# Spreading step log decays on TensorE instead of by DMA, in an mLSTM and two-layer expert kernel

## The chip, the cores and the metric

One core of one Trainium2 chip runs the whole kernel. The metric is the device time of one execution in microseconds (us); lower is better. The runs before: 764.24, 759.52 and 763.80 us, median 763.8.

## The reference

Three layers follow each other. First an mLSTM over 4 batches, 8 heads, 768 tokens and head size 40 (batch x head = 32 rows), with exponential gates:

```python
for t in range(S):
    m_new = np.maximum(f_gate[:, :, t] + m, i_gate[:, :, t])
    f_stab = np.exp(f_gate[:, :, t] + m - m_new)
    i_stab = np.exp(i_gate[:, :, t] - m_new)
    C = f_stab * C + i_stab * einsum('bhd,bhe->bhde', vt, kt)
    n = f_stab * n + i_stab * kt
    y[:, :, t] = sigmoid(o_gate) * (C @ qt) / max(abs(n @ qt), 1)
```

Its 3072 tokens of 320 numbers then go through a mixture of 8 experts (the best of 8 logits picks one, with `relu` between two products and the softmax weight as a factor), and through a dense layer `(h * cos(h)) @ w_out` with `h = x @ w_in` of width 2048.

## The kernel before, in words

**The loop.** The mLSTM is computed in chunks of `L` = 128 tokens. A step `i` of the loop (`for i in range(NT)`, L1051, `NT` = 24) is chunk `c = i // 4` of batch `b = i % 4`, for all 8 heads (4 pairs, `NP`). Inside a chunk the recurrence is written with sums of log decays: `G` holds, for the 32 rows of batch and head, the running sum of the log of `f_stab` since the start of the chunk (`gate_scan`, L256). Step `i` needs, on all partitions, the row of `G` of each of its heads along the tokens: 64 partitions for the even head of a pair, 64 for the odd. This spread row is `gb`, 128 x 4 x 128 numbers.

**Where gb comes from.** For chunk 0, `spread_g` (L329) makes it by f32 matmuls: a column of the identity, repeated 64 times, picks a row of `G` and writes it to 64 partitions of a PSUM bank. For the later chunks `gate_scan` writes `G` to DRAM (`g_d`, L273 to L277), and `load_g` (L232) reads a row back into 64 partitions at once, two DMAs of 128 KB in a step, into one of three SBUF buffers `gb_t`.

**A step's work, in the order in which it is written.** `exps(i + 1)` (L400): eight exponentials of `gb` on ACT make the decay weights `P`, POOL masks them (L418), scales the keys (L422) and the old state (L432). `scores(i)` (L441): PE multiplies keys and queries into banks 0 and 1, DVE multiplies by `P` (L460). `values(i - 1)` (L464): PE makes the state's increment `ps` in bank 6 (L473, columns 0 to 163), the values in bank 4 (L480) and the old state's share in bank 5 (L488); DVE updates the state (L497), adds up and divides (L502 to L524), POOL finishes `y` (L526). Then come the loads of step `i + 3`, the logits of step `i - 3` (L547, bank 3, read by DVE in L548) and the transposes of step `i - 2` (L537, bank 2, copied by ACT to `xT`). Between DVE's operations `fill()` puts single operations of routing and ranking. In two steps of four one piece of `w_in` is decoded (L1723 to L1738), once the step's logits are done.

**What sets the order.** The schedule is by hand: each engine runs its instructions in the order in which they are written, and waits for what they need. All loads of the loop and the stores of finished tiles (`x_d`, L602) are issued by one queue, SP, in this order: gb, kvn, qk (two), v (two), stores. A PSUM bank is one tile `bk[n]`; `qk_t` and `kv_t` have four buffers, so that the load of step `i + 3` goes where step `i - 1` has read. The gates `G`, `gg` and `smask` lie in the space of `w2r`, whose weights come after the loop.

Of the kernel before, what the change touches and what calls it, by code (L numbers as in the profile page):

```python
# [8 lines left out]
F32 = mybir.dt.float32  # L9
F32R = mybir.dt.float32r  # L10
BF16 = mybir.dt.bfloat16
I32 = mybir.dt.int32
U32 = mybir.dt.uint32
AF = mybir.ActivationFunctionType
ALU = mybir.AluOpType
# [4 lines left out]
B, H, S, D = 4, 8, 768, 40  # L20
L = 128
NC = S // L
NP = H // 2
DM = H * D
NTOK = B * S
NT = NTOK // 128
E = 8
# [68 lines left out]
def kernel(  # L96
# [16 lines left out]
    nc = tc.nc  # L113
    V, A, G_, T_ = nc.vector, nc.scalar, nc.gpsimd, nc.tensor
    cp = ctx.enter_context(tc.tile_pool(name="cp", bufs=1))
    dp = ctx.enter_context(tc.tile_pool(name="dp", bufs=1, space=DRAM))
# [1 line left out]

    x_d = dp.tile([NTOK, DM], F32, name="x_d")
    x2_d = dp.tile([NTOK, DM + 1], F32, name="x2_d")  # L120
    g_d = dp.tile([NC - 1, 2, B * NP, L], F32, name="g_d")

    cst = cp.tile([128, C_W], F32, name="cst")
    w_ir = cp.tile([128, 3, DF2], F32, name="w_ir")
# [10 lines left out]
    bk = [pp.tile([128, 512], F32, name=f"bk{i}") for i in range(8)]  # L135
    ident = cst[:, C_ID:C_ID + 128]
# [5 lines left out]
    def pool(stack, name, side="left", bufs=1):  # L142
        return stack.enter_context(tc.tile_pool(name=name, bufs=bufs, side=side, reuse_waits="tile"))

    def many(p, n, name, *shape):
        return [p.tile([128, *shape], F32, name=f"{name}{i}") for i in range(n)]
# [7 lines left out]

    gl = pool(pl_, "gl", "right")
    ge = pool(pe_, "ge")
    NQ, NKV, NG, NPB = 4, 4, 3, 3
    kw_t = many(ge, 3, "kw", NP, 2, 64)
    gb_t = many(ge, 3, "gb", NP, L)
    qk_t = many(ge, 1, "qk", NP, 3 * L)  # L160
    kv_t = many(ge, 1, "kv", 2 * DM + H * DV)
    vb_t = many(ge, 2, "vb", 2, 2, NP * DV)
# [17 lines left out]
    gg, G, smask = (wf[0:B * H, n * S:(n + 1) * S] for n in range(3))  # L180
# [12 lines left out]
    HL, QO = L // 2, 3 * L // 2  # L193
    Z = (slice(0, HL), slice(HL, L))
# [17 lines left out]
    def run(g):  # L212
        for _ in g:
            pass
# [14 lines left out]
            nc.sync.dma_start(out=vb[Z[a], :, a], in_=vpair[i, a])  # L229
        vbt[i] = vb  # L230

    def load_g(i):  # L232
        c, b = divmod(i, B)
        gb = gb_t[i % NG]
        src = g_d[c - 1, :, b * NP:(b + 1) * NP].rearrange("a n t -> a (n t)")
        for a, z in enumerate(Z):
            nc.sync.dma_start(
                out=gb.rearrange("p n t -> p (n t)")[z], in_=src[a:a + 1].to_broadcast([HL, NP * L])
            )
        gbt[i] = gb  # L240

# [14 lines left out]
    def gate_scan(c0, c1, eng):  # L256

        lo, hi = c0 * L, c1 * L
        r, r1 = slice(lo, hi), slice(max(lo, 1), hi)
        r0 = slice(r1.start - 1, hi - 1)  # L260
        V.tensor_tensor_scan(
            out=mm[:, r], data0=fg[:, r], data1=ig[:, r], initial=mm[:, lo - 1:lo] if lo else -1e30,
            op0=ALU.add, op1=ALU.max,
        )
        yield
        V.tensor_tensor(out=gg[:, r1], in0=fg[:, r1], in1=mm[:, r0], op=ALU.add)
        yield
        V.tensor_tensor(out=gg[:, r1], in0=gg[:, r1], in1=mm[:, r1], op=ALU.subtract)
        yield
        V.tensor_tensor_scan(  # L270
            out=G[:, r], data0=smask[:, r], data1=gg[:, r], initial=0.0, op0=ALU.mult, op1=ALU.add
        )
        for a in range(2 if c0 else 0):  # L273
            nc.sync.dma_start(
                out=g_d[c0 - 1:c1 - 1, a].rearrange("c r t -> r c t"),
                in_=G[a:B * H:2, r].rearrange("r (c t) -> r c t", c=c1 - c0),
            )  # L277
        yield
        eng.tensor_tensor(out=aa[:, r], in0=ig[:, r], in1=mm[:, r], op=ALU.subtract)
        yield  # L280
        V.tensor_tensor(out=aa[:, r], in0=aa[:, r], in1=G[:, r], op=ALU.subtract)
        yield
        g3 = G[:, r].rearrange("r (c t) -> r c t", c=c1 - c0)[:, :, L - 1:L]
        V.tensor_tensor(
            out=a2[:, r].rearrange("r (c t) -> r c t", c=c1 - c0), in0=aa[:, r].rearrange("r (c t) -> r c t", c=c1 - c0),
            in1=g3.to_broadcast([B * H, c1 - c0, L]), op=ALU.add,
        )
        yield
        if c0:
            V.tensor_tensor(  # L290
                out=decr[:, c0:c1], in0=g3.to_broadcast([B * H, c1 - c0, B * NP]),
                in1=cst[:B * H, C_DM:C_DM + B * NP].unsqueeze(1).to_broadcast([B * H, c1 - c0, B * NP]),
                op=ALU.mult,
            )
            yield
# [237 lines left out]
    def xpose(i):  # L533
        y = yt[i]
        px = bk[2][:, 0:384]
        for k, c in enumerate(KC):
            T_.transpose(out=px[:, 128 * k:128 * k + 128], in_=y[:, c:c + 128], identity=ident)  # L537
        xT = xT_t[i % 2]
        A.activation(out=xT.rearrange("p k t -> p (k t)"), in_=px, func=AF.Copy)
        xTt[i] = xT  # L540

    def logits(i):
        xT = xTt.pop(i)
        pl = bk[3 if i < NT - 1 else 2][:, 0:E]
        for k in range(3):
            for z in (slice(0, 64), slice(64, 128)):
                T_.matmul(out=pl[z], lhsT=xT[:, k, z], rhs=wg[:, k, :], start=(k == 0), stop=(k == 2))  # L547
        V.tensor_tensor(out=lg[:, i, :], in0=pl, in1=bias[:, i, :], op=ALU.add)  # L548
        fill()
# [493 lines left out]
    nc.sync.dma_start(out=mb, in_=mbias)  # L1043
    nc.sync.dma_start(out=wg, in_=w_gate)
    gs = gate_scan(1, NC, G_)
    for _ in range(GS0):
        next(gs)
    load_qk(3)
# [2 lines left out]
    for i in range(NT):  # L1051
        if i == 0:
            scores(0)
            spread_g(1)
            exps(1)
            spread_g(2)
            for _ in range(5):
                next(gs)
            keep_warm(DUM)
        else:  # L1060
            exps(i + 1)
            if i >= 4 and i < NT - 1 and (i - 4) % B == B - 1 and (i - 4) // B >= SLOW:
                ex_exp((i - 4) // B)
            scores(i)
        if i >= 8 and i % B == 0 and i // B - 2 < SLOW:
            c = i // B - 2
            bg.append(in_turn(rank(c, rank_mm(c)), rows_of(c)))
        if i == NT - 2:
            run(e0)
            early_rows(0)  # L1070
            gather(0)
        if i >= 1:
            values(i - 1)
        if i == 1:
            spread_g(3)
        if 1 <= i <= B:
            keep_warm(DU2, 5)
        if i == 1:
            run(gs)
        if i == 2:  # L1080
            keep_warm(DU3, 2)
            rest()
            token_bias()
        if i == 3:
            natural(1, NC, G, eG, AF.Exp, bk[7])()
        if 3 < i + 3 < NT:
            load_g(i + 3)
            load_kv(i + 3)
            load_qk(i + 3)
            load_v(i + 3)  # L1090
        if i == B:
            nc.sync.dma_start(out=Rf.rearrange("p r e -> p (r e)"), in_=consts[:, C_R:C_END])
        if i == EARLY[0] + 4:
            run(wt[NC - 3])
            run(pf)
            e0 = early_slot(0, star)
            bg.append(e0)
        if i >= 3:
            logits(i - 3)
        if i >= 2:  # L1100
            xpose(i - 2)
        if i >= 3 and (i - 3) % B == B - 1:
            rt = route((i - 3) // B)
            bg.append(rt)
            if SLOW <= (i - 3) // B and i < NT - 2:
                run(rt)
        if i >= 4 and i < NT - 1 and (i - 4) % B == B - 1:
            c = (i - 4) // B
            if c < SLOW:
                run(rt)  # L1110
                ex_exp(c)
            weigh_later(c)
            if i == EARLY[0] + 3:
                pf = pick_first()
                bg.append(pf)
        if i >= 8 and i % B == 0 and i // B - 2 < SLOW:
            run(wt[i // B - 2])
            wq.append(weigh(i // B - 2))
        weigh_some(2 if i > EARLY[0] else 1)
        if 0 < i <= 4:  # L1120
            G_.memset(XS[:, i - 1], 0.0)
        if i >= 2:
            next(sp_ops, None)
        if i == EARLY[0] + 4:
            load_w(0, 0)
        if i == 2:
            next(dec_ops)
        if B <= i < EARLY[0] + 2 and i % B < 2:
            for _ in range(STEPS[i % 2]):
                next(dec_ops, None)  # L1130
        if i == NT - 2:
            for _ in dec_ops:
                pass
            pe_.close()
            pw_ = pool(ctx, "pw")
            wide(pw_, 0)
            hp = [[pw_.tile([128, 2, SLOT], F32R, name=f"{n}{k}") for k in range(2)] for n in ("hh", "hl")]
            for ts, t_ in zip((hh_t, hl_t), hp):
                ts += [t_[k % 2][:, k // 2] for k in range(NHB)]
            load_w(0, 1)  # L1140
# [449 lines left out]
    n = 4 * (DM + 68)  # L1590
# [4 lines left out]
    gp, gv, gg, gs_ = {}, {}, {}, {}  # L1595
# [218 lines left out]
```

## Time and profile before

| | us |
|---|---|
| median of three runs | 763.8 |
| the profiled execution | 765.02 |
| its span (first to last instruction) | 763.3 |
| PE busy | 712.1 (93%) |
| DVE busy | 525.4 (69%) |
| ACT busy | 390.7 (51%) |
| POOL busy | 208.7 (27%) |

The page gives busy time by engine, the span in 40 slices, and the costliest groups of instructions; the trace behind it can be asked for stretches, waits and single instructions. Engines: PE multiplies, PEld loads its weights, DVE and ACT work on vectors, POOL does vector work and indirect DMAs, SP issues DMAs; "SPq" is that queue. The mLSTM loop takes the first 160 us or so, experts and dense layer the rest. The mean granted clock of PE was 0.977 of full speed.

### The profile page before, as it was taken

Reading aid. Unit: us, or ns where it says so; the run is one execution under the profiler, and the core shown is the slowest. Engines: PE = TensorE matmul, PEld = TensorE weight load, DVE = VectorE, ACT = ScalarE, POOL = GpSimd, SP = SyncE. Lnnn points to the kernel's source line nnn. Section 1 sums busy time; section 2 is a strip of 40 time slices with the busy share of each in tenths; the row PEclk is TensorE's granted clock in tenths of the full one; section 3 lists DMA queues with packets and bytes.
Section 4 is the critical chain, followed back from the end, with each engine's and each line's share of the span. In section 5 each row is a group of like instructions: output and inputs, shape, how many; then the busy total and the mean of one; then the engine's idle time right before and its main releaser. Section 6 shows DMA issues by size and latency. Waiting matters only on the chain. (4 is left out here: it accounts for less than half of the span.)

```text
span 763.3 us, 16584 instructions
## 1 busy us (share of the span) xinstructions
PE 712.1 (93%) x5947; PEld 651.7 (85%) x5948; DVE 525.4 (69%) x1206; ACT 390.7 (51%) x903; POOL 208.7 (27%) x280
## 2 busy tenths in 40 slices
PE   8787888789999999999969999999999999999995
PEld 6677777778998999999957899998899998889994
DVE  8788786778445687665648877676677676767662
ACT  4547556544233465454546655555555555555451
POOL 8656566331154442332433002002002001001102
PEclk9899999879999999999999999999999999999998
DMA  7798988871063583422811010010010000000000
GB/s 192 195 230 221 249 234 241 228 214 54 19 194 98 150 251 107 120 75 76 282 44 66 1 36 35 0 35 35 1 35 34 2 1 22 14 1 10 26 1 35
DMA packets 48654, 73.74 MB, mean 97 GB/s; under 512 B 5518, under 2 KB 33776, under 8 KB 48560
## 3 DMA queue, kind: packets, MB, share of 16 engines
q1 hardware_dynamic: 41248, 50.48, 24.3%
q10 hardware_dynamic: 3664, 10.27, 4.7%
q0 software_dynamic: 3648, 11.82, 4.6%
q8 instruction: 49, 0.80, 0.5%
q14 instruction: 45, 0.37, 0.2%
HBM read 89.82 MB, written 12.22 MB: 134 GB/s over the span
## 5 line engine op out<-in xcount | busy, mean ns | idle before, releaser
L1626 ACT ACTIVATE w1r<-w1r 128x512 f32<-128x512 f32 x96 | 60.7, 632 | 104.2 <-DVE w1r L1621 97.9
L1628 DVE TENSOR_TENSOR w1r<-bk,w1r 128x512 f32<-128x512 f32 x96 | 66.3, 691 | 52.5 <-ACT w1r L1626 51.0
L1619 ACT ACTIVATE w1r<-bk,qtr 128x512 f32<-128x512 f32 x96 | 66.0, 687 | 57.8 <-PE bk L1614 55.2
L943 PE MATMUL bk<-XH,WIH 128*128 128x256 f32 x288 | 77.5, 298 | 3.9 <-DVE hl L950 2.5
L1620 DVE TENSOR_SCALAR w1r<-w1r 128x512 f32<-128x512 f32 x96 | 41.2, 429 | 53.0 <-ACT w1r L1619 51.1
L949 ACT ACTIVATE hh<-bk 128x256 fp32r<-128x256 f32 x96 | 36.6, 382 | 75.4 <-PE bk L943 57.8
L1646 PE MATMUL bk<-WOH,gh 128*128 128x320 f32 x228 | 71.0, 311 | 0.0
L1646 PE MATMUL bk<-WOH,gl 128*128 128x320 f32 x228 | 70.6, 310 | 0.0
L1621 DVE TENSOR_TENSOR w1r<-w1r 128x512 f32<-128x512 f32 x96 | 68.3, 711 | 3.3
L1646 PE MATMUL bk<-WOL,gh 128*128 128x320 f32 x228 | 70.4, 309 | 0.0
L950 DVE SCALAR_TENSOR_TENSOR hl<-bk,hh 128x256 fp32r<-128x256 f32 x96 | 40.1, 418 | 42.1 <-ACT hh L949 25.8
L1614 PE MATMUL bk<-XH,WIH 128*128 128x512 f32 x144 | 57.8, 401 | 4.8 <-issue 4.1
L943 PEld LDWEIGHTS bk<-XH,WIH 128*128 128x128 f32 x288 | 55.3, 192 | 7.2 <-DVE hl L950 3.7
L964 PE MATMUL bk<-WOH,hl 128*128 128x320 f32 x192 | 59.9, 312 | 1.2 <-DVE hl L950 1.2
L964 PE MATMUL bk<-WOH,hh 128*128 128x320 f32 x192 | 59.7, 311 | 0.0
L964 PE MATMUL bk<-WOL,hh 128*128 128x320 f32 x192 | 59.4, 309 | 0.0
L970 POOL DMA_INDIRECT x_d<-ys,cinv x26 | 29.3, 1127 | 103.6 <-ACTq L924 74.0
L1614 PE MATMUL bk<-XL,WIH 128*128 128x512 f32 x144 | 57.3, 398 | 0.0
L1614 PE MATMUL bk<-xh,WIH 128*128 128x512 f32 x144 | 56.5, 392 | 0.0
L1614 PE MATMUL bk<-xl,WIH 128*128 128x512 f32 x144 | 56.1, 389 | 0.0
L943 PE MATMUL bk<-XH,WIL 128*128 128x256 f32 x192 | 50.3, 284 | 0.0
L943 PE MATMUL bk<-XL,WIH 128*128 128x256 f32 x288 | 50.2, 284 | 0.0
(381 smaller groups left out, 1986.0 us busy)
## 6 DMA issues: line engine op xcount, KB each, us to landing
w2r<-in_w_dram SPq DMA_DIRECT2D x26, 640.0 KB
w1r<-in_w_dram SPq DMA_DIRECT2D x26, 512.0 KB
w1r<-in_w_dram SPq DMA_DIRECT2D x52, 128.0 KB
kvl<-in_kvn_dram SPq DMA_DIRECT2D x12, 484.0 KB
gb<-g_d SPq DMA_DIRECT2D x40, 128.0 KB
raw<-in_w_out_dram ACTq DMA_DIRECT2D x8, 640.0 KB
qkl<-in_qk_dram SPq DMA_DIRECT2D x24, 160.0 KB
x_d<-y SPq DMA_DIRECT2D x24, 160.0 KB
```

What stands on the lines that cost most here:

```text
L943: T_.matmul(out=ph, lhsT=a, rhs=x_, start=(n == 0), stop=(n == len(mms) - 1))
L949: A.activation(out=hh, in_=ph, func=AF.Relu)
L950: V.scalar_tensor_tensor(out=hl, in0=ph, scalar=0.0, in1=hh.bitcast(F32), op0=ALU.max, op1=ALU.subtract)
L964: T_.matmul(out=py(s, g), lhsT=a[:, gs], rhs=w_, start=(f == 0 and n == 0), stop=(f == NF - 1 and n == 2),)
L970: r = G_.indirect_dma_start(out=dst, out_offset=bass.IndirectOffsetOnAxis(ap=idx, axis=0), in_=src, in_offset=None, bounds_check=NTOK - 1, ...
L1614: T_.matmul(out=ph, lhsT=a, rhs=x_, start=(n == 0), stop=(n == len(mms) - 1))
L1619: A.activation(out=v, in_=gp[T, f], func=AF.Identity, bias=qtr, scale=1.0 / (2 * math.pi))
L1620: V.tensor_scalar(out=kk, in0=v, scalar1=MAGIC, scalar2=MAGIC, op0=ALU.add, op1=ALU.subtract)
L1621: V.tensor_tensor(out=v, in0=v, in1=kk, op=ALU.subtract)
L1626: A.activation(out=v, in_=v, func=AF.Sin, scale=6.283185)
L1628: V.tensor_tensor(out=g, in0=gp.pop((T, f)), in1=v, op=ALU.mult)
L1646: T_.matmul(out=po, lhsT=a[:, js], rhs=w_, start=(f == 0 and n == 0), stop=(f == NFC - 1 and n == 2),)
```

## The change

`g_d`, its writes, `load_g` and the three `gb_t` go. In steps 2 to 4 `g_parts` takes `G` of chunks 1 to 5 apart into three bf16 parts, the value, what is left of it, and what is left of that, stacked in `g3` (96 partitions: three times the 32 rows); `pick` holds the identity three times. `spread_later(i + 2)` then makes `gb` in step `i` in PSUM bank 3: for steps 4 to 6 (`i < FIRST`) by f32 matmuls as in `spread_g`, for the others by one bf16 matmul a head over 96 rows, which adds the three parts up. The logits move from bank 3 to columns 256 to 263 of bank 6 and behind the transposes.

```diff
-    g_d = dp.tile([NC - 1, 2, B * NP, L], F32, name="g_d")
-    NQ, NKV, NG, NPB = 4, 4, 3, 3
+    NQ, NKV, NPB = 4, 4, 3
+    FIRST = B + 3
-    gb_t = many(ge, 3, "gb", NP, L)
+    g3, gm = (ge.tile([128, S - L], BF16, name=n) for n in ("g3", "gm"))
+    pick = ge.tile([128, B * H], BF16, name="pick")
...
-    def load_g(i):
+    def g_parts():
+        g, r = G[:, L:], smask[:, L:]
+        BH = B * H
+        for k in range(3):
+            z = slice(k * BH, (k + 1) * BH)
+            A.activation(out=pick[z], in_=ident[z, z], func=AF.Copy)
+        A.activation(out=g3[0:BH], in_=g, func=AF.Copy)
+        G_.tensor_tensor(out=r, in0=g, in1=g3[0:BH], op=ALU.subtract)
+        yield
+        A.activation(out=gm[0:BH], in_=r, func=AF.Copy)
+        G_.tensor_tensor(out=r, in0=r, in1=gm[0:BH], op=ALU.subtract)
+        yield
+        A.activation(out=g3[BH:2 * BH], in_=gm[0:BH], func=AF.Copy)
+        A.activation(out=g3[2 * BH:3 * BH], in_=r, func=AF.Copy)
+        yield
+
+    def spread_later(i):
+
         c, b = divmod(i, B)
-        gb = gb_t[i % NG]
-        src = g_d[c - 1, :, b * NP:(b + 1) * NP].rearrange("a n t -> a (n t)")
-        for a, z in enumerate(Z):
-            nc.sync.dma_start(
-                out=gb.rearrange("p n t -> p (n t)")[z], in_=src[a:a + 1].to_broadcast([HL, NP * L])
+        gb = bk[3].rearrange("p (n t) -> p n t", n=NP)
+        if i < FIRST:
+            K, of, g = slice(0, B * H), ident, G[:, c * L:(c + 1) * L]
+        else:
+            K, of, g = slice(0, 3 * B * H), pick, g3[0:3 * B * H, (c - 1) * L:c * L]
+        for h in range(H):
+            r = b * H + h
+            T_.matmul(
+                out=gb[Z[h % 2], h // 2], lhsT=of[K, r:r + 1].to_broadcast([K.stop, HL]), rhs=g, start=True, stop=True
             )
         gbt[i] = gb
...
-        for a in range(2 if c0 else 0):
-            nc.sync.dma_start(
-                out=g_d[c0 - 1:c1 - 1, a].rearrange("c r t -> r c t"),
-                in_=G[a:B * H:2, r].rearrange("r (c t) -> r c t", c=c1 - c0),
-            )
...
-        pl = bk[3 if i < NT - 1 else 2][:, 0:E]
+        pl = bk[6][:, 256:256 + E] if i < NT - 2 else bk[3 if i < NT - 1 else 2][:, 0:E]
...
-            load_g(i + 3)
...
+        if 2 <= i < 5:
+            next(gp)
+        if B <= i + 2 < NT:
+            spread_later(i + 2)
+        if i >= 2:
+            xpose(i - 2)
         if i >= 3:
             logits(i - 3)
-        if i >= 2:
-            xpose(i - 2)
```

## Rows read from the trace of the kernel before

**Rows 1.** Stretches from the scores of steps 4, 8, 12, 16, 20 to 23; columns named.
```profile
core 0: us, PE busy (x) PEld busy (x) DVE busy (x) ACT busy (x) POOL busy (x), PEclk, DMA share, GB/s
33.40:60.80 27.40, 21.84 (x364) 19.64 (x365) 20.00 (x55) 14.07 (x46) 15.35 (x25) 0.90 0.96 233
60.80:85.20 24.40, 20.29 (x385) 18.23 (x386) 19.39 (x58) 14.99 (x48) 15.07 (x24) 1.00 0.90 230
85.20:109.10 23.90, 21.66 (x386) 19.63 (x386) 20.10 (x65) 14.26 (x45) 16.11 (x25) 0.93 0.87 239
109.10:133.60 24.50, 21.94 (x392) 19.92 (x392) 15.99 (x61) 14.71 (x47) 14.27 (x25) 0.93 0.89 241
133.60:155.50 21.90, 17.94 (x269) 16.29 (x270) 15.36 (x57) 10.34 (x33) 7.47 (x11) 0.84 0.79 221
```

**Rows 2.** Waits of the loop, 20 to 190 us: total us, times, longest.
```profile
ACT Pl L409 <- DMA gb<-g_d: 20.3, 10, 4.0
...
PE bk L448 <- DMA qk<-in_qk_dram: 8.4, 3, 4.0
```

**Rows 3.** Queue SP, issues of the loads of step 12 and a store.
```profile
75.88 1.67 SPq L237 DMA_DIRECT2D gb<-g_d  x2
...
78.27 0.83 SPq L218 DMA_DIRECT2D qk<-in_qk_dram  x1
...
81.32 1.55 SPq L602 DMA_DIRECT2D x_d<-y  x1
```

**Rows 4.** Timeline of PE, step 9: start us, us, engine, line, tiles, count.
```profile
67.29 0.68 PE L448 MATMUL bk<-qkb 128*128 128x128 f32 x4 [1.08 <-DVE rk L661]
...
69.21 0.62 PE L473 MATMUL bk<-kv,kw 128*64 128x41 f32 x16
...
71.32 0.23 PE L488 MATMUL bk<-M,qk 128*64 128x82 f32 x1
...
72.17 0.61 PE L448 MATMUL bk<-qkl 128*128 128x128 f32 x4
```

**Rows 5.** Timeline of DVE, steps 8 to 10, state update and logits.
```profile
65.47 0.66 DVE L497 TENSOR_TENSOR Ml<-Mc,bk 40x164 f32<-40x164 f32 x2 [1.59 <-PE bk L488]
...
69.08 0.16 DVE L548 TENSOR_TENSOR lg<-bk,bias 128x8 f32<-128x8 f32 x1
...
71.60 0.65 DVE L497 TENSOR_TENSOR M<-Mc,bk 40x164 f32<-40x164 f32 x2
...
74.55 0.12 DVE L548 TENSOR_TENSOR lg<-bk,bias 128x8 f32<-128x8 f32 x1
...
77.25 0.65 DVE L497 TENSOR_TENSOR M<-Mc,bk 40x164 f32<-40x164 f32 x2
```

**Rows 6.** Timeline at the start of the loop: SP and PE.
```profile
20.74 1.28 SPq L274 DMA_DIRECT2D g_d<-w2r  x2
...
26.51 0.86 SPq L218 DMA_DIRECT2D qk<-in_qk_dram  x1
...
33.41 1.19 PE L448 MATMUL bk<-qk 128*128 128x128 f32 x4 [3.96 <-DMA qk<-in_qk_dram]
```

**Rows 7.** Timeline, prices of kinds: f32 spread, exponentials, subtraction, copy.
```profile
7.50 1.97 ACT L409 ACTIVATE P<-bk,aw 128x128 f32<-128x128 f32 x8 [0.42 <-PE bk L332]
...
9.50 1.96 PE L332 MATMUL bk<-w2r,cst 32*64 32x128 f32 x32
...
16.97 1.54 POOL L279 TENSOR_TENSOR w1r<-w1r 32x640 f32<-32x640 f32 x1
...
66.31 0.49 ACT L539 ACTIVATE xT<-bk 128x384 f32<-128x384 f32 x1 [0.82 <-PE bk L537]
...
68.47 2.24 ACT L409 ACTIVATE Pl<-gb,aw 128x128 f32<-128x128 f32 x8 [0.43 <-DMA gb<-g_d]
```

**Rows 8.** Timeline: ACT held in step 20, PE held at the first slot.
```profile
136.80 1.02 ACT L601 ACTIVATE y<-y,gate 128x320 f32<-128x320 f32 x2 [3.41 <-DVE gate L595]
...
165.71 1.33 PE L844 MATMUL bk<-cst,XS 128*128 128x128 f32 x5 [3.44 <-DMA XS<-x_d,inv]
```

More of the change, by code (lines that the diff above doesn't have):

```diff
@@ L1045 @@
     gs = gate_scan(1, NC, G_)
+    gp = g_parts()
     for _ in range(GS0):
```

## The prediction

> **What bounds the kernel now.** I read the page first, then the time in stretches, the waits, and the timelines of the queue (SP), PE and DVE for one step.
>
> The page's slices show two kernels in one. From about 200 us on PE is busy nearly all the time and nothing there is touched. Before that lies the mLSTM loop, where a step issues scores, values, transposes and logits, and only this part can move. [Rows 1] cut it at the starts of the scores of steps 4, 8, 12, 16, 20 and 23: 27.4, 24.4, 23.9, 24.5 us for four steps each, 21.9 for three; 122.1 us for 19 steps, 6.43 us a step. No engine is full in these rows (PE 0.80 to 0.91 of the first four stretches), but the DMA share is 0.87 to 0.96. So the loop waits, and the transfers are the first suspect.
>
> [Rows 2] say for what: PE waits before its scores for the qk loads (the row is the largest of three such), ACT before its exponentials for gb, the spread log decays. ACT's wait costs less than it looks: what it makes is used a whole step later. PE's wait is on the path.
>
> [Rows 3] say why qk is late: the loads of step 12 are handed to SP in step 9 (67.3 to 72.2), but SP starts them at 75.88 (gb) and 78.27 (qk), and a store of a finished tile leaves at 81.32. SP runs a step and more late. gb takes the largest single part of that: 1.67 us here, and by the tiles' shapes gb is 256 of the step's 1384 KB (kvn 484, qk 320, v 164, x_d 160), 18%.
>
> [Rows 4] is one step in which PE was not held: scores from 67.29, state products from 69.21, the last product ends 71.55, logits, transposes, next scores at 72.17. So PE needs 4.88 us of the 6.43: 1.92 for scores, 2.34 for values, 0.62 for the rest. [Rows 5] is DVE beside it: from L497 to the end of L548, its last work of a step, 3.07 us (71.60 to 74.67), and 3.77 in a step with ranking (65.47 to 69.24).
>
> **The change part by part.**
>
> *Removed: gb's transfers.* Per step two issues, 1.1 to 1.7 us of SP's 6, and 18% of the bytes. At the same rate the DMA share of the last full stretches falls from 0.89 to about 0.73, and SP from all of 6 us to some 4.7. Loads are then late only when their buffer is: qk's is free when the values of the step before last are done, two steps ahead. I cost PE's waits for qk at zero afterwards. Next in line are PE itself and DVE.
>
> *Removed: the write of g_d and the first wait for it.* [Rows 6]: SP issues g_d at 20.74, must see it land before the first gb, and starts the qk load of step 4 at 26.51; PE stands 3.96 us before 33.41 for it. With SP free at 20.74 only kvn stands ahead of that load, so it starts about 5 us sooner.
>
> *Added: the spread on PE.* The same spread in f32 ran in the first steps as 16 instructions for its eight products, 32 instructions (two steps' worth) in 1.96 us [rows 7]: 0.98 us a step, 61 ns an instruction. The three f32 spreads (of steps 4, 5, 6, made in steps 2, 3, 4) are costed at that. A bf16 spread is eight products of the same 128 columns, over 96 rows in place of 32; no row shows that form. Bounds: 0.49 us if each is one such instruction, 0.98 if each costs what two do. I take 0.49, the f32 row having two instructions a product only. In all 3 x 0.98 + 17 x 0.49 = 11.3 us of PE work.
>
> *Added: the three parts.* Two subtractions of 32x640 on POOL at 1.54 us each [rows 7], four copies of that size on ACT, some 0.8 us each by ACT's xT copy (384 elements, 0.49 us [rows 7]), and three small ones, in steps 2 to 4: near 5 us of ACT over three steps. They are covered by the time in which ACT stood waiting for gb; without that cover a step's share (at most 2 us) would delay a spread. Bounds 0 and 2 us, taken as 0.
>
> *Moved: the exponentials' source.* They read PSUM in place of SBUF. The first steps already did; 8 take 1.97 us there and 2.24 from gb [rows 7]: no cost. But there is now one buffer in place of three. Spread i+2 cannot start before the exponentials of i+1 have been read; behind it in PE's queue stand transposes, logits and the next scores. In the step of [rows 4] the exponentials end at 70.71 (68.47 + 2.24 [rows 7]) and the spread would come at 71.55: 0.8 us to spare. In step 20 ACT is held for the gate until 136.80 [rows 8], and I charge 1.2 us there.
>
> *Moved: logits.* They go behind the transposes and into bank 6, at column 256, where the state products use columns 0 to 163. If the two are ordered as one tile, PE's state products must wait for DVE's read of the logits (L548), near the end of DVE's step, and the logits for L497. In [rows 4, 5] scores start at 72.17 and take 1.92, so the next state products come at 74.09, while L548 ends at 74.67: a wait of 0.6 us, with the rest of values, the spread, transposes, logits and the next scores queued behind it. The Trainium skill, "PSUM — Partial Sum Buffer", section "PSUM bank collisions raise a hardware error", says two engines must be kept apart by bank and quadrant, also at different columns, which speaks against this move; no run here shows it yet. I take the wait as real, since the columns share a tile; bounds 0 and 0.6 us in a plain step.
>
> *The new step.* PE alone: 4.88 + 0.49 + some 0.3 for hand-overs = 5.65. Loop over bank 6: L548, 2.34 of products, L497 to L548 3.07, hand-overs 0.15 = 5.6; with ranking 3.77, so 6.3; with the second half of the decoding DVE is 2.58 late at L497 (74.67 to 77.25), 5.8. Four steps: 6.3 + 5.8 + 5.65 + 5.65 + 0.3 (routing, not priced by rows) = 23.7.
>
> *Sum*, against the profiled execution's 765.0 us (span 763.3):
> - to the scores of step 4: 3.96 of wait gone, 1.96 of f32 spread and 0.3 of hand-over in its place: -1.7
> - steps 4 to 7: 27.4 to 4 x 5.65 + 0.5 (the third f32 spread) + 0.5 (decoding, room) = 23.6: -3.8
> - steps 8 to 19: 72.8 to 3 x 23.7 = 71.1: -1.7
> - steps 20 to 22: 21.9 to 3 x 5.65 + 1.2 (the gate) + 1.5 (the early slot's products and sums, an estimate) = 19.6: -2.3. The granted clock was 0.84 there [rows 1], part of it at the lower level of 1.2 GHz after waits; with few waits I count on the upper level
> - the first slot: PE stands 3.44 us at 165.71 for a gather [rows 8] whose rows and weights come through the same late SP: -2
> - room that ideal steps leave out (0.15 us in each of 19): +2.9
>
> Together -8.6, called -9: 756 for the profiled execution. The median of the runs shown is 1.2 below it, so 755.
>
> **The rivals.**
>
> *Larger gain.* Bank 6 costs nothing because DVE, too, runs freer once loads and stores are early, and the full clock holds all through (0.84 to 0.93 in four stretches now). Steps of 5.65: another 3 us in steps 8 to 19 and the 3 us of room: 763.8 - 15 = 749. For it: DVE is busy only 0.65 to 0.84. Against: one in four DVE steps is long.
>
> *Little gain.* The loop over bank 6, or the one over bank 3, holds each step at about 6.1, so the middle gives nothing and only the ends win (1.7 + 2): -4, 760. For it: steps 8 to 19 already run at 72.8 / 12 = 6.07 with the waits. The same time comes out if qk stays late because its buffer, not the queue, sets it.
>
> *Slower.* The single gb buffer: ACT late makes PE late, whose transposes make ACT late. The loop is spread 0.49, transposes some 0.4 of the 0.62 after the values [rows 4], then ACT from the copy of the transposes to the last exponential, 4.4 us (66.31 to 70.71 [rows 7]): 5.3, some 5.5 with hand-overs. It decides when ACT is held 1 us more in most steps, 6.5 a step; held 1.5 us, or with PE's clock falling in the gaps, 7.0, which is 19 x 0.57 less the ends' 3.7: +7, 771. For it: [rows 8] show ACT held 3.41 us once. Against: that hold is of one step, and the gb waits that filled ACT's gaps go.
>
> **How the numbers follow.** Forecast 0.42 (its own range 750 to 760), larger gain 0.17, little gain 0.28, slower 0.13. About 1% (7.6 us) is what a measurement can tell: below 756.2 is faster. Of the forecast's 0.42 some 0.36 lies there, with the larger gain 0.53; same 0.06 + 0.28 = 0.34; slower 0.13. The range runs from 745 to 765: it leaves out the slower rival and a twentieth below.
>
> **What would show it.** Right: no wait of PE's scores for qk; ACT's exponentials wait for nobody's DMA; DMA share near 0.73 to 0.8; the stretch from scores 8 to scores 20 at 68 to 72 us against 72.8; L332's bf16 successors at 0.5 us a step; waits of the state products on L548 near 0.5 us. Wrong: waits of the spread on L409 in most steps; steps of ranking over 7 us; qk still waited for; clock below 0.9 in the middle.

## The result and the profile after

The changed kernel took 753.09 us (median of six runs, 751.96 to 757.24) against 762.77 us for the kernel before, a ratio of 0.9885 with a 95% interval of 0.9845 to 0.9925. The profiled execution took 751.96 us, the shortest of the six; its span is 750.2 us, and the mean granted clock of PE was 0.983. Here and below, medians are over all executions, while ratios leave out one slow execution each of four experiments (bytes_on_sp, gb_on_act, all_f32, bytes_and_wait), over 1.5% above the fastest of its kernel.

The same stretches as in [rows 1], from the scores of steps 4, 8, 12, 16, 20 to 23 (PE, PEld, DVE, ACT and POOL busy, granted clock, DMA share, GB/s):

```profile
35.40:57.50 22.10, 21.96 (x409) 19.19 (x406) 16.99 (x47) 14.13 (x49) 17.20 (x27) 1.00 0.67 194
57.50:80.10 22.60, 22.37 (x421) 19.51 (x417) 19.59 (x67) 13.67 (x49) 15.40 (x25) 1.00 0.77 219
80.10:102.80 22.70, 22.45 (x422) 19.56 (x420) 19.74 (x67) 13.43 (x47) 15.80 (x25) 1.00 0.78 207
102.80:126.40 23.60, 22.51 (x426) 19.63 (x424) 18.23 (x67) 13.57 (x48) 13.19 (x22) 1.00 0.80 218
126.40:145.60 19.20, 17.99 (x292) 15.71 (x289) 14.44 (x54) 9.80 (x34) 7.76 (x11) 0.91 0.77 226
```

The 19 steps take 110.2 us where they took 122.1. PE is busy for 22.0 to 22.5 us of each of the first four stretches, at the upper level of its clock (2.4 GHz) in all of them: in the loop, too, PE is now nearly full. The DMA share of these four fell from between 0.87 and 0.96 to between 0.67 and 0.80.

The waits of the loop, 15 to 190 us (total us, times, longest us); the first three rows are of PE's weight loads (PEld), the fourth of PE's matmuls:

```profile
PEld bk L565 <- DVE Ml L515: 2.9, 7, 1.1
PEld bk L565 <- DVE M L515: 2.3, 8, 0.3
PEld bk L491 <- DVE lg L566: 0.5, 3, 0.2
PE bk L260 <- ACT P L427: 1.2, 1, 1.2
```

The waits for qk of [rows 2] do not occur between 33 and 160 us. What stands in their place is small: the logits (L565, before L547) wait for the state update (L515, before L497), the state products (L491) three times for the logits' reader, and one spread (L260) waits for ACT.

PE in step 9 and at the start of step 10, which answers to [rows 4] (start us, us, line, tiles, shapes, count):

```profile
63.36 0.71 PE L466 MATMUL bk<-qkb 128*128 128x128 f32 x4
...
65.51 0.67 PE L491 MATMUL bk<-kv,kw 128*64 128x41 f32 x16
...
67.69 0.44 PE L260 MATMUL bk<-g,pick 96*64 96x128 bf16 x5
68.06 0.55 PE L555 MATMUL bk<-cst,y 128*128 128x128 f32 x3
68.66 0.52 PE L565 MATMUL bk<-wg,xT 128*64 128x8 f32 x12
69.11 0.71 PE L466 MATMUL bk<-qkl 128*128 128x128 f32 x4
```

A step runs from 63.36 to 69.11: 5.75 us. The four steps from 57.50 took 5.86, 5.75, 5.49 and 5.54 us, the first with ranking; before, the same four took 6.49, 4.88, 5.09 and 7.96, so the steps without a wait were shorter than now, and the waits in the others cost more than that. DVE beside it answers to [rows 5]:

```profile
62.20 0.66 DVE L515 TENSOR_TENSOR Ml<-Mc,bk 40x164 f32<-40x164 f32 x2 [1.45 <-PE bk L506]
65.30 0.16 DVE L566 TENSOR_TENSOR lg<-bk,bias 128x8 f32<-128x8 f32 x1
67.94 0.66 DVE L515 TENSOR_TENSOR M<-Mc,bk 40x164 f32<-40x164 f32 x2
70.75 0.11 DVE L566 TENSOR_TENSOR lg<-bk,bias 128x8 f32<-128x8 f32 x1
```

DVE's read of the logits (L566) ends at 65.46, and PE's state products (L491) start at 65.51; the state update (L515) ends near 68.60, and the logits start at 68.66. Both orders across bank 6 are kept in the trace, although the two uses share no column. That agrees with the Trainium skill, "PSUM — Partial Sum Buffer", section "PSUM bank collisions raise a hardware error", by which accesses are to be kept apart by bank and quadrant and not by address; here the order is the program's, in which the bank is one tile.

Queue SP, the loads of step 12 and the store behind them, for [rows 3]:

```profile
70.59 0.46 SPq L225 DMA_DIRECT2D kv<-in_kvn_dram  x1
71.15 0.82 SPq L220 DMA_DIRECT2D qk<-in_qk_dram  x1
...
74.18 0.53 SPq L620 DMA_DIRECT2D x_d<-y  x1
```

qk leaves at 71.15 rather than 78.27, in a loop that started 2 us later. A better measure is the time from the start of the scores of the step in which the loads are written (step 9 here): 7.8 us now, 11.0 before; over the loads of steps 7 to 22 the mean is 7.4, and was 11.6. Ahead of its kvn loads (L225) SP now stands for 26.1 us, in 16 waits, until DVE has read the buffer.

**Where the time went.** By the starts of the scores, one profiled execution each:

| us | to scores 4 | 4 to 8 | 8 to 20 | 20 to 23 | after scores 23 |
|---|---|---|---|---|---|
| before | 33.4 | 27.4 | 72.8 | 21.9 | 607.8 |
| after | 35.4 | 22.1 | 68.9 | 19.2 | 604.6 |
| forecast of the difference | -1.7 | -3.8 | -1.7 (+2.9 of room for the loop) | -2.3 | -2 |
| measured | +2.0 | -5.3 | -3.9 | -2.7 | -3.2 |

The measured terms add up to 13.1 us, the difference of the two profiled executions; the medians differ by 9.7, so over 3 us of the table are the chance of these two.

The waits also show in PE's clock. Before, four steps ran in part at its lower level (1.2 GHz): steps 4, 12, 17 and 22, each begun behind a wait of PE, of 3.96, 2.92, 1.77 and 3.15 us, the last of them for DVE (L522) and the others for qk. Waits of 2.80 and 1.94 us ahead of steps 8 and 6 were followed by no fall. In the changed kernel one step is left, step 21 (the last row):

```profile
33.41:40.20 6.79, 6.79 (x79) 6.20 (x80) 2.31 (x6) 2.59 (x9) 4.67 (x9) 0.59 0.99 248
85.22:91.89 6.67, 6.67 (x101) 6.14 (x101) 3.52 (x14) 2.82 (x10) 5.49 (x10) 0.74 0.94 250
116.23:122.67 6.44, 6.44 (x96) 6.00 (x97) 3.23 (x13) 2.59 (x9) 4.30 (x8) 0.74 0.87 209
147.17:155.51 8.34, 8.34 (x95) 7.77 (x96) 2.21 (x7) 2.60 (x9) 2.82 (x4) 0.59 0.75 216
```

```profile
133.16:139.55 6.39, 6.39 (x91) 5.54 (x87) 5.18 (x21) 3.60 (x13) 2.50 (x4) 0.73 0.80 234
```

Beside steps at 1.00 (4.9 to 5.1 us for a plain one, 6.05 for step 22 of the changed kernel) these lost some 1.4 to 2.3 us each, an estimate. So a wait ahead of the scores cost more than its own length wherever the clock fell behind it.

### The profile page after: what moved, and what is told of

Its sections match the earlier page's. It is cut to its first block, busy times and chain, and to the rows that moved or that the text cites. A ratio compares the mean times of both kernels' runs of the same rounds, so it can differ in the third digit from the quotient of the medians.

```text
span 750.2 us, 16869 instructions
## 1 busy us (share of the span) xinstructions
PE 719.6 (96%) x6131; PEld 655.5 (87%) x6132; DVE 522.3 (70%) x1206; ACT 387.1 (52%) x910; POOL 210.1 (28%) x282
```

## The experiments

The theory was the prediction's: loads came late because SP ran a step late, and because gb's bytes filled the transfers. Its two halves can be separated, and each has a rival: that neither matters and ACT's wait for gb was the price. A second group asks what holds the step now: PE's work, or the loop through bank 6. Runs that have the same median of the kernel before beside them ran on one chip.

**The bytes and the issues put back, together and apart.** All on the changed kernel; `idle_t` is a buffer of gb's size that nothing reads:

```
+    def idle_load(i):                     # bytes_on_sp: the 2 x 128 KB of gb
+        t = idle_t[i % 3].rearrange("p n t -> p (n t)")
+        for a, z in enumerate(Z):
+            nc.sync.dma_start(out=t[z, 0:512], in_=consts[2 * i + a:2 * i + a + 1, 0:512].to_broadcast([HL, 512]))
...
+            idle_load(i + 3)              # where load_g(i + 3) stood
```

In issue_on_sp 8 stands for 512, so that SP issues as often and next to no bytes move; in bytes_on_act `A.dma_start` stands for `nc.sync.dma_start`.

> The changed kernel, with the two 128 KB transfers of a step put back on queue SP at their old place (same packets, from the constants, into three buffers that nobody reads). Theory: the gain came from taking these transfers away, so the loop waits for qk again and the DMA share is back at 0.87 or more: 761 to 766 us. Rival: the gain came from ACT no longer waiting for gb, which nobody does here either: 752 to 756.

> The changed kernel with two transfers a step on SP at the old place, but of 2 KB in all in place of 128 KB each: SP's issue time without the bytes. If SP's time was what made loads late: 761 to 766 us, with qk waits. If the bytes were: 753 to 755, no qk waits. Rival (ACT's gb wait): 752 to 756.

> The changed kernel with the two 128 KB transfers a step issued by ACT's queue: the bytes without SP's time, and some 1.1 us of ACT a step. If the bytes made loads late: 761 to 766 us, DMA share 0.87 or more and qk waits. If SP's issue time did: 753 to 755. Rival (ACT's gb wait): 752 to 756.

Measured beside 766.83 us for the kernel before: bytes_on_sp 763.86 us, ratio 0.9969 (0.9930 to 1.0009); issue_on_sp 757.78, 0.9889 (0.9835 to 0.9943); bytes_on_act 770.19, 1.0045 (1.0013 to 1.0078), above the range expected. The issues alone cost nothing that these runs can tell: issue_on_sp has the ratio of the changed kernel (0.9885), known to some 4 us. The bytes cost 6.1 us, bytes_on_sp less issue_on_sp. A stretch of four steps, first issue_on_sp, then bytes_on_sp:

```profile
59.50:82.20 22.70, 22.46 (x422) 19.56 (x420) 19.69 (x67) 13.76 (x49) 15.49 (x25) 1.00 0.71 192
```

```profile
60.00:82.80 22.80, 22.53 (x422) 19.59 (x419) 19.82 (x67) 13.96 (x49) 15.61 (x25) 1.00 0.95 242
82.80:106.70 23.90, 22.55 (x417) 19.52 (x417) 19.40 (x66) 13.51 (x46) 15.63 (x25) 1.00 0.89 243
```

With the bytes back the DMA share is 0.95, as before, and yet the first of these stretches is not longer; the second loses 1.2 us against the changed kernel's 22.7. The waits for qk are small there, while on ACT's queue they are large (waits of bytes_on_sp, then of bytes_on_act):

```profile
PE bk L472 <- DMA qkl<-in_qk_dram: 1.1, 3, 0.4
```

```profile
PE bk L472 <- DMA qk<-in_qk_dram: 4.6, 2, 4.1
```

So at 0.95 PE is hardly held up by the transfers as they come from SP, and is where they come at other times: behind the wait of 4.1 us, ahead of step 8, that step took 8.8 us at a granted clock of 0.61. The loop of bytes_on_sp is 2.1 us longer than that of the changed kernel (112.3 against 110.2); the rest of its 6 us lies before step 4 and behind the loop, where single executions of one kernel differ by as much, and is not placed by these runs.

**The kernel before with gb on ACT's queue.** One word of `load_g`: `A.dma_start` for `nc.sync.dma_start`.

> The kernel before, with the loads of gb (they are used here) issued by ACT's queue in place of SP's; nothing else changed. If SP's issue time was the cause: 752 to 757, since PE has no spread to do. If the bytes were: 760 to 765. Rival: if ACT's wait for gb was the cause, no change, 761 to 766.

Measured beside 766.83 us: 767.69, ratio 1.0016 (0.9975 to 1.0057). Moving gb's issues off SP gives nothing. It does not make SP earlier either: qk leaves 11.6 us after the start of the step in which its load is written, as before, since SP now stands for gb's transfers. So this run does not show what an earlier SP would be worth. PE still waits for qk, and ACT and SP stand in waits that the trace puts down to gb (three of the rows):

```profile
PE bk L448 <- DMA qkb<-in_qk_dram: 6.4, 3, 2.9
ACT xT L539 <- DMA gb<-g_d: 6.9, 2, 3.5
SPq L229 <- DMA gb<-g_d: 9.0, 4, 3.9
```

**ACT's wait put back too.** bytes_on_sp, and ahead of the exponentials ACT reads one column of the idle load:

```
+        if i > 3:
+            A.activation(out=seen, in_=idle_t[i % 3][:, 0, 0:1], func=AF.Copy)
```

> As bytes_on_sp (0.997 of before, loop of 112.4 us from scores 4 to scores 23), and ACT reads one column of what the step's two transfers brought before its exponentials, in some 0.2 us: the wait for gb without its use. If that wait, with ACT's later work and SP's stores behind it, is what held the loop besides the traffic: loop of 118 us or more, 1.005 to 1.02 of before. Rival, that traffic alone counts: loop within 2 us of bytes_on_sp, 0.995 to 1.002.

> The changed kernel once more, beside the three others: 0.985 to 0.992 of before by both theories; its loop from scores 4 to scores 23 at 110 to 111 us if the profiled run of it was typical, its scores of step 4 anywhere from 33 to 38 us if the 2 us lost at the start were the chance of one execution.

Measured beside 765.11 us: the changed kernel 755.23, ratio 0.9874 (0.9847 to 0.9901), with scores of step 4 at 37.0 us and a loop of 110.3; bytes_and_wait 760.86, 0.9940 (0.9910 to 0.9969). The expectation that this brings back the time of before was wrong: it brings back 5.6 of 9.9 us. ACT's wait is there:

```profile
ACT seen L431 <- DMA idle<-in_consts_dram: 13.0, 10, 2.4
```

It costs no more than the bytes alone did (0.9969 and 0.9940, with intervals that overlap). In the profiled executions steps 8 to 19 take 68.9 us in the changed kernel, 71.0 with the bytes, 73.7 with bytes and wait, 72.8 before. But the 2.7 us that the wait seems to add there are those of one step, step 8, which began 1.15 us late for qk and ran at a lower clock; bytes_on_sp has it at 5.86 us, and the other eleven steps take 64.9 and 65.1:

```profile
60.22 0.79 PE L475 MATMUL bk<-qk 128*128 128x128 f32 x4 [1.15 <-DMA qk<-in_qk_dram]
```

```profile
60.22:69.01 8.79, 8.74 (x108) 7.67 (x108) 3.85 (x16) 3.14 (x14) 4.34 (x8) 0.61 0.88 217
```

So no run shows that ACT's wait costs the loop anything by itself. What bytes and wait do not bring back is at the loop's two ends: steps 4 to 7 take 23.5 us against 27.4, steps 20 to 22 17.8 against 21.9. Steps 4 and 22 of the kernel before, at a clock of 0.59, lie there. The write of `g_d` and the wait for it, ahead of step 4, and the wait for DVE's L522, ahead of step 22, are the candidates; neither was tried alone, and some 4 us of the gain stay without a shown cause.

**What holds the step now: PE's work.** all_f32 makes every spread in f32 (`FIRST = NT`), which adds PE work and nothing else to a step. pairs gives each bf16 matmul two heads, with `pick` widened to [128, B*H, L//2]:

```
+            for n in range(NP):
+                r = b * H + 2 * n
+                T_.matmul(out=gb[:, n], lhsT=pick[K, r:r + 2].rearrange("p r w -> p (r w)"), rhs=g, start=True, stop=True)
```

> The changed kernel with every spread by f32 products of one part (16 instructions, 1.09 us) in place of bf16 on three (8 instructions, about 0.55 us); g_parts still runs. If PE alone bounds the loop now: 17 steps x 0.55 = 9 us over the changed kernel, so about the time of before. Rival, that a loop through DVE and bank 6 or ACT and bank 3 bounds it: under 4 us over the changed kernel.

> The changed kernel with the bf16 spread as four products of 128 weight columns (both heads of a pair at once) in place of eight of 64; ACT widens the pick matrix to 64 columns a row in steps 2 to 4. If PE bounds the loop: 17 steps x 0.2 to 0.27 us = 3.5 to 4.5 us under the changed kernel, less what ACT's three copies of 32x2048 cost early. Rival (another loop bounds): no change, within 1.5 us.

Measured beside 764.9 us: all_f32 761.33, ratio 0.9967 (0.9944 to 0.9990); pairs 756.62, 0.9884 (0.9841 to 0.9927). The profiled execution of all_f32 took 770.71 us and lost most of the excess before step 4 (44.2 us, at a clock of 0.70), so only its later steps, at 1.00, are read. PE is full there, busy in all of the two steps shown:

```profile
82.20:94.60 12.40, 12.40 (x227) 10.87 (x226) 10.25 (x30) 6.61 (x23) 8.28 (x14) 1.00 0.89 236
```

A step takes 6.2 us rather than 5.5, and the spread 1.09 rather than 0.41: what PE is given, the step takes. The form of the matmul decides the change; in f32 about two thirds of the gain go. pairs changes nothing, where 3.5 to 4.5 us were expected: from its first score to its first transpose a step takes 4.44 us with the eight narrow matmuls (69.11 to 73.55) and 4.46 with the four wide ones (71.90 to 76.36). By their starts the wide ones take less, 0.24 us up to the transposes (76.12 to 76.36), but the narrow ones begin among the last products with the old state, and the wide ones behind them. The changed kernel, then pairs:

```profile
73.18 0.44 PE L260 MATMUL bk<-g,pick 96*64 96x128 bf16 x5
73.55 0.55 PE L555 MATMUL bk<-cst,y 128*128 128x128 f32 x3
```

```profile
71.90 0.71 PE L478 MATMUL bk<-qkl 128*128 128x128 f32 x4
76.12 0.40 PE L272 MATMUL bk<-g,pick 96*128 96x128 bf16 x4
76.36 0.50 PE L567 MATMUL bk<-cst,y 128*128 128x128 f32 x3
```

In step 20, where PE has waited, none of the changed kernel's spread mixes with another kind:

```profile
131.89 0.41 PE L260 MATMUL bk<-g,pick 96*64 96x128 bf16 x8 [1.21 <-ACT P L427]
```

**What holds the step now: bank 6.** bank7 puts the logits into columns 256 to 263 of bank 7, which ranking uses, logits_first puts them back ahead of the transposes, in bank 6:

```
-        pl = bk[6][:, 256:256 + E] if i < NT - 2 else ...      # bank7
+        pl = bk[7][:, 256:256 + E] if i < NT - 2 else ...
```

```
+        if i >= 3:                                             # logits_first
+            logits(i - 3)
         if i >= 2:
             xpose(i - 2)
-        if i >= 3:
-            logits(i - 3)
```

> The changed kernel with the logits in bank 7 in place of bank 6. If sharing bank 6 with the state products costs what the waits of the logits on the state update show (6 us in all): 3 to 6 us under the changed kernel. Rival, that other waits take their place or PE has that time to spare: within 1.5 us of it.

> The changed kernel with the logits ahead of the transposes again, still in bank 6. The logits then reach PE 0.5 us sooner, while the state update that they wait for ends where it did: about 0.3 us more waiting in each of 16 steps, 3 to 6 us over the changed kernel. Rival, that the order is of no weight: within 1.5 us of it.

Measured beside 764.9 us: bank7 752.67, ratio 0.9871 (0.9817 to 0.9925); logits_first 754.02, 0.9884 (0.9823 to 0.9944). Both have the time of the changed kernel, where 3 to 6 us less and 3 to 6 us more were expected. bank7 shortens a plain step from 5.5 to 5.4, but a step with ranking now takes 6.5 rather than 5.9, since the logits wait for ranking's reader (L677), and once, in step 19, ranking waits 2.7 us for the logits' reader:

```profile
PE bk L661 <- DVE lg L566: 2.7, 1, 2.7
PE bk L565 <- DVE tot L677: 2.0, 3, 0.7
```

logits_first makes the wait for the state update longer, and a plain step 5.8:

```profile
PE bk L565 <- DVE M L515: 4.2, 8, 0.6
PE bk L565 <- DVE Ml L515: 4.1, 7, 0.9
```

Its loop still ends as early (110.1 us), since steps 20 to 22 took 16.4 rather than 19.2; step 21 took 4.6 at a clock of 1.00, rather than 6.4 at 0.73. The place of the logits moves waits about; it is worth 0.1 to 0.3 us a plain step, and nothing in the whole.

**Taking the cause of that wait away.** The state is updated in place, so the update (L515) waits until PE has read the old state (L506, the last of three groups of products in `values`): the 1.45 us in the DVE rows above. old_state_first moves the old state's products ahead of the values':

```
+        pi = bk[5][:, 0:H * DV].rearrange(...)      # old state's share, with its loop
         po = bk[4 if i < NT - 1 else 6][:, 0:H * DV].rearrange(...)
         ...
-        pi = bk[5][:, 0:H * DV].rearrange(...)
```

old_state_pairs does this and pairs at once.

> The changed kernel with the product with the old state (bank 5) ahead of the values (bank 4) in PE's order. DVE may then update the state 1 us sooner, so that the logits in bank 6 no longer wait for it. If that loop holds the plain step at 5.5 us beside PE's own 5.4: steps of 5.4, 1 to 2 us under the changed kernel. Rival, PE alone bounds: no change.

> Both: the old state's product first, and the spread as four products of 128 weight columns. By the theory of two equal bounds (PE and the loop over bank 6) taking both down gives what neither gave alone: plain steps of 5.1 to 5.3 us, 4 to 6 us under the changed kernel. Rival, that a third loop (ACT and bank 3, or DVE) stands right behind them: steps of 5.4 or more, within 2 us.

Measured beside 765.11: old_state_first 747.34 us, ratio 0.9778 (0.9748 to 0.9808), 1.0% under the changed kernel's 755.23 on the same chip, with intervals far apart; old_state_pairs 752.23, 0.9847 (0.9814 to 0.9880). The gain of the first was expected at 1 to 2 us and came out at 7.9. In its profile PE has no idle time left in eight steps, and of the waits for the update two of 0.2 us are left:

```profile
58.30:80.20 21.90, 21.90 (x421) 19.42 (x419) 19.89 (x65) 13.66 (x49) 15.47 (x25) 1.00 0.81 216
80.20:102.10 21.90, 21.90 (x422) 19.44 (x418) 20.15 (x66) 13.32 (x47) 15.51 (x25) 1.00 0.80 215
```

```profile
PEld bk L565 <- DVE M L515: 0.2, 1, 0.2
PEld bk L565 <- DVE Ml L515: 0.2, 1, 0.2
```

Its steps take 5.4 us, 5.7 with ranking, and the loop from step 4 to step 23 105.1 us rather than 110.2. Of these 5.0 us 1.5 are step 21, at a clock of 1.00 here and of 0.73 in the changed kernel, and 1.0 is step 19, where the longest wait of the logits stood. The other 3 us lie behind the loop and are seen in single executions only (602.2 us against 604.6 and 606.6). It beats both kernels. The edit also lets DVE's next operation (L520, which reads bank 5) start sooner; these runs do not part that from the state update. old_state_pairs, expected 4 to 6 us under the changed kernel, is 3.0 under it and 4.9 above old_state_first: its steps take 5.3 us, but it has 608.8 us behind the loop, as pairs has 608.6. Both keep a `pick` 64 times as wide and make it with larger copies. Whether that costs the time is open, since single executions of the other kernels have from 601.7 (bank7) to 611.1 us (bytes_on_act) there.

## Why the prediction was right, and where its steps were wrong

The total was right, 755 us for 753.09, and so was the call of a gain of over 1% (though the interval reaches to 0.9925). For the profiled execution 8.6 us less were forecast and 13.1 measured. Point by point:

**What bounded the loop.** Right that it was no engine but waits, for the larger part on transfers, and that PE's own work would be next. Wrong in the step "[Rows 3] say why qk is late": SP's lateness was taken as the cause, with the bytes as its companion. issue_on_sp has its qk loads leave 9.4 us after the start of the step in which they are written (mean of steps 7 to 22), which is half of the way from 7.4 in the changed kernel back to 11.6 before, and loses no time (0.9889). bytes_on_sp has 10.0, hardly later, and loses 6.1 us. So SP was late, but what a late issue cost depended on how long the transfers behind it took; the bytes are the price. "ACT's wait costs less than it looks" holds: its 20.3 us put back beside the bytes, in part (13.0), leave the bytes' cost where it was (5.6 us). The sum counts the clock only in steps 20 to 22; behind waits PE also ran below its upper level in steps 4, 12 and 17, and in step 22 the wait ahead was for DVE.

**The bf16 spread.** Taken as 0.49 us, measured as 0.41 where nothing mixes with it; the upper bound of 0.98 is excluded. No row of before had shown that form, so the choice of the bound was a guess with a reason. f32 spreads took 1.09 where 0.98 was charged. This choice decided the case: all_f32, which is nearly the upper bound made real, stands at 0.9967, inside the 1%.

**The step.** Forecast 5.65, measured 5.5; with ranking 6.3 against 5.9. DVE's 3.77 us of the ranking step were put into the loop in full; measured, the step lost only 0.4 to a plain one.

**Bank 6.** The order across the bank is real, and the products do start where DVE's read ends, but the wait was at the other end: the state products stood still for 0.5 us in three times, where 0.5 in each step was expected, and the logits waited for the state update, 5.2 us in 15 waits of PE's weight loads. The loop was drawn as going through DVE alone (L497 to L548); it also goes through PE's reading of the old state, which the forecast left out. old_state_first, which cuts that edge, is what shows it.

**One gb buffer.** Right. The spread waits for the exponentials once, 1.21 us in step 20, where 1.2 was charged; the slower rival's waits in most steps are absent.

**The start.** Wrong in sign: +2.0 us in place of -1.7. PE's wait of 3.96 us for qk [rows 6] is gone, and qk is issued earlier, at 21.89. But PE now gets to the scores of step 4 late by itself: its clock fell to the lower level twice, once behind a wait of 1.85 us, where the kernel before has the upper level from 14 to 32 us with a wait of 1.6 us in the same place; and the two f32 spreads ahead of step 4 cost 1.09 each, one waiting for ACT. PE's rows, then the two stretches:

```profile
13.58 0.77 PE L466 MATMUL bk<-qkb 128*128 128x128 f32 x4 [1.85 <-DMA qkb<-in_qk_dram]
...
26.61 1.09 PE L260 MATMUL bk<-w2r,cst 32*64 32x128 f32 x16 [0.48 <-ACT decay L383]
```

```profile
14.00:17.40 3.40, 3.40 (x41) 2.85 (x39) 3.33 (x4) 2.25 (x9) 2.92 (x3) 0.51 1.02 233
27.80:31.00 3.20, 3.20 (x19) 2.70 (x18) 2.83 (x5) 2.55 (x12) 2.06 (x4) 0.50 0.78 228
```

At the upper level the work of these 6.6 us would take half as long, so by this estimate the clock accounts for some 3.3 us of the 3.7 between forecast and result. In the other profiled executions but that of all_f32 step 4 started at 34.9 to 38.7 us, at 37.0 in the repeat of the changed kernel and at 37.7 also in gb_on_act, which has the PE work of the kernel before. So one execution of each does not size the start, and -1.7 was a false precision.

**Room and the other terms.** The +2.9 us of room was not needed: steps 4 to 7 gave 5.3 (forecast 3.8) and steps 8 to 19 3.9 (forecast 1.7), and beside the missing waits the granted clock held at 1.00 in all four stretches, where three of those in [rows 1] had 0.90 to 0.93. The end gave 3.2 where 2 was charged, and 1.2 in the repeat (606.6 us). The loop's 11.9 us against some 5 to 8 forecast was closer to the rival of the larger gain; the start took the difference back. That the total agreed better than its terms did was luck.

## What to carry to other kernels

Work that moves from transfers to the engine that is nearly full pays only if its form is cheap there: the same spread as one bf16 product of three exact parts a head won 1.2%, and as f32 products a third of that. When a queue runs late, test issues and bytes apart before blaming either; moving the issues to another queue does not part them. Where a step's engine has just become the bound, look for a read that holds up an in-place update: putting it first cost one moved block and gave another 1.0%. And look at the clock of the step behind a wait: in bytes_and_wait 1.15 us of waiting were followed by a step that took 2.9 us more.

## What was not expected of the hardware

- Eight products of 64 output columns over 96 rows with 128 bf16 columns took 0.41 us from the first start to the last end, and four of 128 output columns 0.40. The wide ones' starts span less, 0.24 us up to the next kind, yet the step gained nothing from them (4.46 against 4.44 us from scores to transposes), since the narrow ones start among the products ahead of them. In f32 the spread over 32 rows took 16 instructions for its eight products and 1.09 us.
- 256 KB more a step, which no computation uses, took the DMA share of the loop's stretches from 0.67 to 0.80 up to 0.86 to 0.95 and cost 5.6 to 6.1 us of the run, while the issues that carry them cost nothing on SP. With the same bytes issued from ACT the time rose by another 6.3 us (770.19 against 763.86), and SP was no earlier for it: its qk loads left 10.8 us after the step's start, against 10.0.
- PE's granted clock stayed at its upper level in most stretches in which PE was full; step 21 of the changed kernel is an exception, full at 0.73 behind a wait of 1.21 us in step 20, while step 21 of old_state_first, behind 1.16 us in the same place, kept 1.00. The same wait at the start of the loop, 1.85 us in one execution and 1.6 in the other, was followed by 1.2 GHz from 14.0 to 17.4 us in the first and by no fall in the second.
